# A gated attention and MLP decode step: w2's first half loaded behind wo, and the result summed as two 288-column rows

## The chip, the cores and the metric

The kernel runs on one NeuronCore of a Trainium2 chip. The metric is the device time of one execution in microseconds (us). The kernel before takes 131.41 us, the median of 3 runs (131.40 to 131.53).

## The reference

One token, width 576. Branch A is attention over the last 4096 positions of a cache with 32 query heads, 16 key heads and head width 128. Branch B is an MLP of width 4608 with GELU. A sigmoid gate mixes them.

```python
def _A_ref(x, k_cache, v_cache, wq, wo):          # Hq=32, Hkv=16, Sk=32768, Dh=128
    W = min(4096, max(256, Sk // 4))
    q = (x @ wq).reshape(B, Sq, Hq, Dh).transpose(0, 2, 1, 3)
    k = jnp.repeat(k_cache[:, :, Sk - W:, :], 2, axis=1)
    v = jnp.repeat(v_cache[:, :, Sk - W:, :], 2, axis=1)
    p = softmax(jnp.einsum("bhqd,bhkd->bhqk", q, k) * (Dh ** -0.5))
    o = jnp.einsum("bhqk,bhkd->bhqd", p, v)
    return o.transpose(0, 2, 1, 3).reshape(B, Sq, Hq * Dh) @ wo
def _B_ref(x, w1, b1, w2, b2):
    h = gelu(jnp.einsum("bsd,df->bsf", x, w1) + b1)
    return jnp.einsum("bsf,fd->bsd", h, w2) + b2
g = sigmoid((x * gate_w).sum(-1, keepdims=True))
return g * _A_ref(...) + (1 - g) * _B_ref(...)    # (1, 1, 576), bfloat16
```

## The kernel before

Everything is a product of one row with a large matrix, so the kernel is mostly a stream of loads: w1, wq, four groups of keys (`k_t`), four groups of values (`v_t`), `w2`, `wo`. All of these loads are issued on SP, one after the other. The order of the issues in the program is the order in which the bytes are asked for. A tile that takes over the place (tag) of another one is only loaded when the last reader of the old tile is done.

Each group holds 4 key heads. DVE transposes the keys in two halves (L550), TensorE makes the scores (L572), ACT the exponentials (L609), DVE transposes the probabilities (L621). Then `value_products(g)` (L662) multiplies with group g of the values, `own_sums(g)` (L676, L686, DVE) keeps each head's own part, and `outputs(g)` (L697) collects the heads' columns in `o_ps`. After the last group DVE scales them with the gate into `om` and `om_t` (L769, L778), TensorE turns them into the layout in which wo's rows lie (`ov_ps`, L786 and L793), DVE and ACT copy that to `ov` and `ov_tail` (L802, L804).

The helper `queue("pe", ...)` fixes the order of work on TensorE by hand: each call is issued behind the one before it. The same is done for DVE.

The result is summed in PSUM in the tile `y_ps`. `y_add(vec, row)` multiplies one column of a vector (128 partitions) with one row block of a weight matrix (128 x 576) and adds the 576 products to the sum. It does so as two matmuls in two column groups of the array: columns 0 to 271 on partition 0, columns 272 to 575 on partition 32 in another bank. A "row" in this text is one such call: 36 of them for `w2` (vector `gt`), 31 for `wo` (vector `ov`), 4 for the rest of wo (`wo_tail`, vector `ov_tail`). In the program's order these are: six w2 rows behind the last `value_products`, two behind `outputs(3)`, ten behind the `ov_ps` matmuls, the four tail rows, one dummy matmul (512 columns in fp32 into the unused `spare`, L815), the 31 wo rows, and the second 18 w2 rows.

`w2` is loaded in two halves of 18 rows. The first half is one load (L646, 2592 KB), issued between the second and the third `v_t`; the second half is four loads (L757) of 10, 5, 2 and 1 rows, behind `wo` (L752, 4464 KB). At the end ACT and DVE cast the two parts of the sum into `out_row` on one partition (L828, L829), and SP stores it (L830).

Of the kernel before, what the change touches and what calls it, by code (L numbers as in the profile page):

```python
# [9 lines left out]
FP32 = mybir.dt.float32  # L10
BF16 = mybir.dt.bfloat16
I32 = mybir.dt.int32
ACT = mybir.ActivationFunctionType
ALU = mybir.AluOpType
# [4 lines left out]
def kernel(  # L19
# [15 lines left out]
    nc = tc.nc  # L35

    P = 128
    D = 576
# [9 lines left out]
    NJ = FH // P  # L48
    NF = 2 * NJ
    NI = 2 * D // P  # L50
    QH = Hq * Dh // 2
    DH = 272
    SCALE = 1.0 / (Dh**0.5)

    def first_load_ahead(nc):
# [153 lines left out]
    const = ctx.enter_context(tc.tile_pool(name="const", bufs=1))  # L209
# [3 lines left out]
    ps_y = ctx.enter_context(tc.tile_pool(name="ps_y", bufs=1, space=bass.MemoryType.PSUM))  # L213
# [29 lines left out]
    c0 = 0  # L243
    for base, pattern, keep in (
# [6 lines left out]
        n = 1  # L251
# [8 lines left out]
        out=is0[:], in0=low[:], scalar1=0.0, scalar2=None, op0=ALU.is_equal  # L260
    )
    alt = is0[:, 0 : 2 * NI].rearrange("p (i t) -> p i t", t=2)
    ones = const.tile([P, P], FP32, name="ones")
# [12 lines left out]
        out=at31,  # L276
        in_=at31,
# [8 lines left out]
        out=hi5[:],  # L286
        in_=ones[:, 0:5],
# [7 lines left out]
        out=hi5[:],  # L295
        in_=hi5[:],
# [6 lines left out]
    c0 = 2 * NI  # L303
    hi16 = const.tile([P, 16], FP32, name="hi16")
    nc.gpsimd.tensor_scalar(
        out=hi16[:], in0=is0[:, c0 : c0 + 16], scalar1=-SCALE, scalar2=None, op0=ALU.mult
# [6 lines left out]
        out=row_of,  # L313
        in_=row_of,
# [9 lines left out]
        out=foreign[:],  # L324
        in_=foreign[:],
# [11 lines left out]
        out=xdup.rearrange("p (d t) -> p d t", t=2),  # L337
        in_=x_row.rearrange("p (d o) -> p d o", o=1).to_broadcast([1, D, 2]),
    )
    xs_ps = ps_m.tile([P, NI, 1], FP32, name="xs_ps", tag="m")  # L340
    for i in range(NI):
        nc.tensor.matmul(  # L342
            xs_ps[:, i, :],
            lhsT=xdup[:, i : 2 * D : NI],
            rhs=ident[0:1, 0:1],
            start=(i == 0),
            stop=(i == NI - 1),
            skip_group_check=True,
        )
    nc.vector.tensor_tensor(  # L350
        out=x2[:, :, 0:2], in0=xs_ps[:].to_broadcast([P, NI, 2]), in1=alt, op=ALU.mult
# [5 lines left out]
        out=junk_row,  # L357
        in0=x_row,
        in1=gw_row,
# [15 lines left out]
    b2g = const.tile([1, D], FP32, name="b2g")  # L375
# [2 lines left out]
    nc.scalar.activation(out=gh[:, 0, :], in_=hi5[:], func=ACT.Copy, scale=g_t[:, 0:1])  # L378


    y_ps = ps_y.tile([64, 1024], FP32, name="y_ps")
    y_out = (y_ps[0:1, 0:DH], y_ps[32:33, 512 : 512 + D - DH])

    def y_add(vec, row, start=False, stop=False):
        for s in range(2):
            last = nc.tensor.matmul(  # L386
                y_out[s],
                lhsT=vec,
                rhs=row[:, DH:D] if s else row[:, 0:DH],
                start=start,  # L390
                stop=stop,
                skip_group_check=True,
            )
        return last

    y_add(ones[0:1, 0:1], b2g[0:1, :], start=True)


    QZ = 24
# [30 lines left out]
    for c0, src, q in ((0, h_s[0], 2), (1024, h_s[1], 2), (2048, h_m, 4)):  # L430
        n = 1024 if q == 2 else 256
        nc.vector.transpose(  # L432
            out=turned[:, c0 : c0 + n],
            in_=src[:].rearrange("p (q l j) -> p q j l", q=q, l=32),
# [3 lines left out]
    for j0, j1, b0 in ((0, 16, 0), (16, NJ, 64)):  # L438
        nc.tensor.matmul(
            hp_ps[:, :, :, j0:j1].rearrange("p q t j -> p q j t"),  # L440
            lhsT=same32,
            rhs=turned_t[:, b0 : b0 + 4 * (j1 - j0), :],
            start=(j0 == 0),
            stop=True,
            skip_group_check=True,
        )
    hacc = const.tile([P, NF], FP32, name="hacc")
    for q in range(4):
        quad = slice(32 * q, 32 * q + 32)
        nc.scalar.copy(  # L450
            out=hacc[quad], in_=hp_ps[quad, q, :, :].rearrange("p t j -> p (t j)")
# [6 lines left out]
        out=poly[:],  # L458
        in0=z2[:],
# [12 lines left out]
    gt = const.tile([P, NF], BF16, name="gt")  # L472
    nc.vector.scalar_tensor_tensor(
        out=gt[:], in0=hacc[:], scalar=omg[:, 0:1], in1=r_t[:], op0=ALU.mult, op1=ALU.mult
# [11 lines left out]
    for c in range(2):  # L486
        nc.vector.transpose(  # L487
            out=q_turned[:, 1024 * c : 1024 * c + 1024],
            in_=q_s[c][:].rearrange("p (h l b) -> p h b l", l=32, b=2),
# [4 lines left out]
        lhsT=same32,  # L494
        rhs=q_turned[:].rearrange("p (h j l) -> p h j l", h=16, j=4)[:, :, :, 0:2],
        start=True,
        stop=True,
    )
    for b in range(4):
        quad = slice(32 * b, 32 * b + 32)  # L500
        at = QZ + 32 * b
# [4 lines left out]
            out=diag[:, :, :, 0:8],  # L506
            in_=qj_ps[quad].rearrange("p j g q -> p g j q"),
# [11 lines left out]
    p_t = const.tile([P, 32, 32], BF16, name="p_t")  # L519
# [6 lines left out]
    def queue(engine, emit):  # L526
        if engine in issued:
            with tc.issue_after(issued[engine].ins):
                issued[engine] = emit()
        else:  # L530
            issued[engine] = emit()

    def load(name, tag, cache, g):
        tile_ = big.tile([P, NCK, Dh], BF16, name=name, tag=tag)
        src = cache[0, HB * g : HB * g + HB, Sk - W : Sk, :].rearrange(
            "b (k c) d -> k b (c d)", k=NKP
        )
        nc.sync.dma_start(out=tile_[:].rearrange("p c d -> p (c d)"), in_=src)
        return tile_
# [103 lines left out]
    w2_t = big.tile([P, NF, D], BF16, name="w2_t", tag="B")  # L643
    w2_src = B_w2.rearrange("(b p j) n -> p b j n", b=2, j=NJ)
    v_t = [load("v_t", "CD"[g], A_v_cache, g) for g in range(2)]
    nc.sync.dma_start(out=w2_t[:, 0:NJ, :], in_=w2_src[:, 0])  # L646
    v_t.append(load("v_t", "A", A_v_cache, 2))
    wo_src = A_wo.rearrange("(h d) n -> h d n", d=P)
    tail = wo_src[:, 4 * RW : P, :]
    for h0, h1, at, k in ((0, 16, 0, 4), (16, Hq, 32, 4)):  # L650
        load_tail = nc.sync.dma_start(
            out=wo_tail[at : at + h1 - h0].rearrange("h j n -> h (j n)"),
            in_=tail[h0:h1].rearrange("h j n -> h (j n)"),
# [40 lines left out]
    def outputs(g):  # L694
        queue(
            "pe",
            lambda: nc.tensor.matmul(  # L697
                o_ps[:, 8 * g : 8 * g + 8],
                lhsT=summed[g][:],
                rhs=same8[:, 0:8],  # L700
                start=True,
                stop=True,
            ),
        )
# [9 lines left out]
        out=ls[:],  # L714
        in0=same8[:, 0:8].rearrange("p (o q) -> p o q", o=1).to_broadcast([P, NG, 8]),
        in1=sums[:].to_broadcast([P, NG, 8]),
        op=ALU.mult,
# [5 lines left out]
    spare = acc3[:, 512:1024]  # L723
# [5 lines left out]
            t_ps, lhsT=ones[:], rhs=ls[:].rearrange("p g q -> p (g q)"), start=True, stop=True  # L729
# [7 lines left out]
        out=rgh[:],  # L737
        in0=rg[:].to_broadcast([P, Hq, 5]),
        in1=gh[:].to_broadcast([P, Hq, 5]),
        op=ALU.mult,  # L740
# [12 lines left out]
        out=wo_t[:].rearrange("p r n -> p (r n)"),  # L753
        in_=wo_src[:, 0 : 4 * RW, :].rearrange("h (a r) n -> h a (r n)", a=4),
    )
    for j0, j1 in ((0, 10), (10, 15), (15, 17), (17, 18)):
        nc.sync.dma_start(out=w2_t[:, NJ + j0 : NJ + j1, :], in_=w2_src[:, 1, j0:j1, :])  # L757

    def w2_rows(f0, f1):
        for f in range(f0, f1):  # L760
            queue("pe", lambda: y_add(gt[:, f : f + 1], w2_t[:, f, :]))

    w2_rows(0, 6)
    outputs(3)
    o_all = o_ps.rearrange("p (h o) -> p h o", o=1)
    om = const.tile([P, Hq, 4], BF16, name="om")
# [3 lines left out]
            out=om_t.rearrange("p (u h) -> p u h", u=2)[:, :, 0:16],  # L770
            in0=o_ps.rearrange("p (u h) -> p u h", u=2),
            in1=rgh[:, :, 4].rearrange("p (u h) -> p u h", u=2),
            op=ALU.mult,
# [5 lines left out]
            out=om[:], in0=o_all.to_broadcast([P, Hq, 4]), in1=rgh[:, :, 0:4], op=ALU.mult  # L779
        ),  # L780
    )
    w2_rows(6, 8)
    ov_ps = ps_m.tile([P, RO + 4], FP32, name="ov_ps", tag="m")
    queue(
        "pe",
# [4 lines left out]
    for a in range(4):  # L790
# [4 lines left out]
                lhsT=om[:].rearrange("p h a -> p (h a)"),  # L795
                rhs=at31[:, a, :],
                start=(a == 0),
                stop=(a == 3),
# [4 lines left out]
    ov_tail = const.tile([48, 4], BF16, name="ov_tail")  # L803
    nc.scalar.copy(out=ov_tail[:], in_=ov_ps[0:48, RO : RO + 4])  # L804

    w2_rows(8, NJ)
    late = [(ov_tail, j, wo_tail[:, j, :]) for j in range(4)]
    late.append(None)
    late += [(ov, r, wo_t[:, r, :]) for r in range(RO)]
    late += [(gt, f, w2_t[:, f, :]) for f in range(NJ, NF)]  # L810
    for n, item in enumerate(late):
        if item is None:
            queue(
                "pe",
                lambda: nc.tensor.matmul(  # L815
                    spare,
                    lhsT=ones[:],
                    rhs=p_t[:].rearrange("p c k -> p (c k)").bitcast(FP32),
                    start=True,
                    stop=True,  # L820
                ),
            )
            continue
        vec, at, row = item
        queue("pe", lambda: y_add(vec[:, at : at + 1], row, stop=(n == len(late) - 1)))

    out_row = const.tile([1, D], BF16, name="out_row")
    nc.scalar.copy(out=out_row[:, DH:D], in_=y_out[1])  # L828
    nc.vector.tensor_copy(out=out_row[:, 0:DH], in_=y_out[0])  # L829
    nc.sync.dma_start(out=out.rearrange("a b d -> (a b) d"), in_=out_row[:])  # L830


# [28 lines left out]
```

## Time and profile before

| what | value |
|---|---|
| median of 3 runs | 131.41 us (131.40 to 131.53) |
| the profiled execution | 131.67 us |
| span of its records | 130.3 us |
| mean granted TensorE clock | 0.817 |
| DMA | 53.67 MB, mean 412 GB/s over the span |
| busy TensorE, VectorE, ScalarE, GpSimd | 79.3, 61.0, 11.5, 10.0 us |

The span runs from the first to the last instruction that the profiler recorded; the execution is 1.4 us longer. PE is TensorE, PEld its weight loads, DVE VectorE, ACT ScalarE, POOL GpSimd, SP SyncE, and SPq its DMA issues. A group such as `L386 PE MATMUL ... x72` gives a line of the kernel, an engine, an operation and how many there are. "PEclk" is the clock that TensorE was granted, as a share of the full one. A line in the timeline gives start, duration, engine, line and operation, and in brackets the idle time ahead of it with what ended it.

### The profile page before, as it was taken

The page shows a single profiled execution, that of the slowest core. Times are in us where ns is not written, and L with a number is a line of the kernel's source. Part 1 is how long each engine was busy: PE and PEld are TensorE (multiplying, and loading weights), DVE is VectorE, ACT ScalarE, POOL GpSimd, SP SyncE. Part 2 cuts the span into 40 slices and gives each one's busy share as a digit, 9 for nine tenths or more (in the row PEclk, how much of TensorE's full clock was granted, in tenths as well). Part 3 has the DMA queues.
Part 4 walks back from the last instruction along what each step waited for, and adds up shares of the span by engine and source line. Part 5 has one row for each costly group of instructions (what it writes and reads, how often), then busy time and mean ns, then how long its engine had stood idle before and what let it go on. Part 6 is the DMA issues. An engine that isn't in the chain of part 4 may idle for free.

```text
span 130.3 us, 1142 instructions
## 1 busy us (share of the span) xinstructions
PE 79.3 (61%) x538; PEld 26.2 (20%) x412; DVE 61.0 (47%) x50; ACT 11.5 (9%) x27; POOL 10.0 (8%) x32
## 2 busy tenths in 40 slices
PE   0003899297106996859949946995300840789794
PEld 0003012110100221211211210132200320245572
DVE  0030006215199769999999995145900050051001
ACT  3032100300300000030003003003000000000001
POOL 7009800100000000000000000000010000000000
PEclk9999999658755799985999995599655577579999
DMA  7999999899899999989989989999989999898970
GB/s 249 404 437 432 475 419 475 364 473 473 362 453 473 408 402 473 433 382 473 443 372 473 453 362 473 391 458 443 443 372 477 444 392 475 384 493 356 407 294 15
DMA packets 2503, 53.67 MB, mean 412 GB/s; under 512 B 286, under 2 KB 418, under 8 KB 708
## 3 DMA queue, kind: packets, MB, share of 16 engines
q1 hardware_dynamic: 2490, 53.61, 96.3%
q8 instruction: 3, 0.05, 0.2%
q10 hardware_dynamic: 10, 0.01, 0.0%
HBM read 53.62 MB, written 0.00 MB: 412 GB/s over the span
## 4 chain that ended last, share of the span: by engine, by line
DMA 60%; DVE 21%; PE 13%; issue 5%; ACT 0%; DVEq 0%
DMA k_t<-in_A_k_cache_dram 31%; DMA wo_t<-in_A_wo_dram 25%; DVE kt L550 15%; PE y_ps L386 5%; PE s_ps L572 5%; DMA rows<-in_A_x_dram 5%; DVE m L588 3%; DVE pt L621 2%; PE s_ps L662 1%; PE acc L662 1%; DVE mr L591 1%; ACT out_row L828 0%; PE mt_ps L597 0%; DVE negm L605 0%; DVEq L550 0%
## 5 line engine op out<-in xcount | busy, mean ns | idle before, releaser
L572 PE MATMUL s_ps<-kt,qz_flat 128*128 128x512 bf16 x128 | 35.3, 436 | 15.1 <-DVE kt L550 8.3
L550 DVE STREAM_TRANSPOSE kt<-k_t 128x4096 f32<-128x4096 f32 x8 | 35.3, 4432 | 4.8 <-DMA k_t<-in_A_k_cache_dram 4.8
L662 PE MATMUL s_ps<-v_t,pt 128*32 128x512 bf16 x96 | 9.1, 547 | 12.0 <-DMA v_t<-in_A_v_cache_dram 12.0
L572 PEld LDWEIGHTS <-qz_flat 128*128 128x128 bf16 x64 | 7.2, 112 | 40.6 <-issue 40.4
L676 DVE TENSOR_TENSOR own<-s_ps,is 128x512 f32<-128x512 f32 x3 | 2.1, 688 | 18.9 <-PE s_ps L662 18.9
L609 ACT ACTIVATE p_t<-s_ps,negm 128x1024 bf16<-128x1024 f32 x4 | 4.5, 1114 | 50.0 <-DVE negm L605 50.0
L662 PEld LDWEIGHTS <-pt 128*32 128x32 bf16 x128 | 3.7, 117 | 17.5 <-DMA v_t<-in_A_v_cache_dram 12.2
L342 PE MATMUL xs_ps<-ident,rows 1*128 1x1 bf16 x9 | 0.6, 189 | 10.8 <-POOL ident masks.py:199 10.8
L407 PE MATMUL s_ps<-w_t,x 128*32 128x512 bf16 x36 | 6.0, 611 | 1.6 <-DVE x L350 1.6
L588 DVE TENSOR_REDUCE m<-s_ps 128x1 f32<-128x1024 f32 x4 | 4.8, 1195 | 3.9 <-PE s_ps L572 3.9
L386 PE MATMUL y_ps<-w_t,gt 128*1 128x272 bf16 (+1 forms) x72 | 6.3, 304 | 0.0
L407 PE MATMUL s_ps<-wq_t,x 128*32 128x512 bf16 x36 | 4.9, 619 | 2.2 <-DMA wq_t<-in_A_wq_dram 2.2
L621 DVE STREAM_TRANSPOSE pt<-p_t 128x1024 bf16<-128x1024 bf16 x4 | 4.9, 1224 | 2.7 <-ACT p_t L609 2.7
L432 DVE STREAM_TRANSPOSE turned<-s_ps 128x1024 f32<-128x1024 f32 x2 | 2.5, 1249 | 7.3 <-PE s_ps L407 7.2
L829 DVE CAST out_row<-y_ps 1x272 bf16<-1x272 f32 x1 | 0.4, 429 | 10.2 <-PE y_ps L386 10.2
L713 POOL TENSOR_TENSOR ls<-is,sums 128x32 f32<-128x32 f32 x1 | 0.2, 240 | 63.9 <-ACT p_t L609 63.9
L697 PE MATMUL mt_ps<-is,summed 128*128 128x8 f32 x8 | 2.0, 319 | 4.6 <-DVE summed L686 4.6
L386 PE MATMUL y_ps<-wo_t,ov 128*1 128x272 bf16 (+1 forms) x62 | 4.2, 286 | 0.8 <-DMA wo_t<-in_A_wo_dram 0.8
L356 DVE CUSTOM_DVE_ANT_0 rows<-rows 1x576 bf16<-1x576 bf16 x1 | 0.7, 746 | 8.3 <-DMA rows<-in_gate_w_dram 8.3
L386 PEld LDWEIGHTS <-gt 128*1 128x1 bf16 x72 | 4.0, 89 | 1.9 <-issue 0.7
L686 DVE TENSOR_REDUCE summed<-own 128x128 f32<-128x512 f32 x4 | 4.2, 1044 | 0.1
L487 DVE STREAM_TRANSPOSE q_turned<-s_ps 128x1024 f32<-128x1024 f32 x2 | 2.4, 1228 | 3.8 <-PE s_ps L407 3.8
(83 smaller groups left out, 51.9 us busy)
## 6 DMA issues: line engine op xcount, KB each, us to landing
k_t<-in_A_k_cache_dram SPq DMA_DIRECT2D x4, 4096.0 KB, 33.9
v_t<-in_A_v_cache_dram SPq DMA_DIRECT2D x4, 4096.0 KB, 22.8
wq_t<-in_A_wq_dram SPq DMA_DIRECT2D x1, 4608.0 KB, 25.0
wo_t<-in_A_wo_dram SPq DMA_DIRECT2D x1, 4464.0 KB
w_t<-in_B_w_dram SPq DMA_DIRECT2D x1, 2880.0 KB, 14.4
w_t<-in_B_w_dram SPq DMA_DIRECT2D x1, 2592.0 KB, 23.6
w_t<-in_B_w_dram SPq DMA_DIRECT2D x1, 2304.0 KB, 8.3
w_t<-in_B_w_dram SPq DMA_DIRECT2D x1, 1440.0 KB
```

What stands on the lines that cost most here:

```text
L386: last = nc.tensor.matmul(y_out[s], lhsT=vec, rhs=row[:, DH:D] if s else row[:, 0:DH], start=start, stop=stop, skip_group_check=True,)
L407: nc.tensor.matmul(last[n][32 * g : 32 * g + 32], lhsT=vec, rhs=part(n), start=start and g0 == 0, stop=g0 + 4 + g >= len(pieces), skip_gro ...
L432: nc.vector.transpose(out=turned[:, c0 : c0 + n], in_=src[:].rearrange("p (q l j) -> p q j l", q=q, l=32),)
L487: nc.vector.transpose(out=q_turned[:, 1024 * c : 1024 * c + 1024], in_=q_s[c][:].rearrange("p (h l b) -> p h b l", l=32, b=2),)
L550: lambda: nc.vector.transpose(out=kt[g, f][:].bitcast(FP32), in_=keys.rearrange("p c d -> p (c d)").bitcast(FP32),),
L572: last = nc.tensor.matmul(s_ps[g][:, u * 512 : (u + 1) * 512].rearrange("p (c k) -> p c k", k=32), lhsT=qz(g, j, 2 * f + half), rhs=kv[:, ...
L588: queue("dve", lambda: nc.vector.reduce_max(out=m1[:], in_=s_ps[g][:], axis=AX.X))
L609: nc.scalar.activation(out=p_t[:].rearrange("p c k -> p (c k)"), in_=s_ps[g][:], func=ACT.Exp, bias=negm[:, 0:1], scale=SCALE, accum_out=s ...
L621: lambda: nc.vector.transpose(out=pt[:, g, :, :].rearrange("p c q -> p (c q)"), in_=p_t[:].rearrange("p c k -> p (c k)"),),
L662: last = nc.tensor.matmul(acc[g][32 * (c % 4) : 32 * (c % 4) + 32, :], lhsT=pt[:, g, c, :], rhs=v_t[g][:, c:NCK:32, :], start=(c < 4), sto ...
L676: lambda: nc.vector.tensor_tensor(out=own[:], in0=acc[g].rearrange("p (c d) -> p c d", c=4), in1=same_c.rearrange("p (c o) -> p c o", o=1) ...
L686: lambda: nc.vector.tensor_reduce(out=summed[g][:], in_=own[:].rearrange("p c d -> p d c"), axis=AX.X, op=ALU.add,),
```

## The change

- The first half of `w2` is no longer loaded between the second and the third `v_t`, but behind `wo` and ahead of the four pieces of the second half. Its 18 rows move behind the wo rows on TensorE, so none is left among the last attention steps.
- Of the dummy matmuls there are now four of 512 columns ahead of the wo rows, one of 512 between wo and w2, and one of 256 between the halves of w2.
- The sum lies as two rows of 288 columns on partitions 0 and 32 of one bank (`y_ps`). The last eight w2 rows go through `y_late`: columns 0 to 151 of each row are added to `y_ps`, columns 152 to 287 go into a second bank (`yb_ps`). Ahead of them ACT copies columns 152 to 287 of the sum so far into `y_part`.
- The first of the late rows (and the bias row) use 32 equal weight columns, so that all 32 partitions of a group are written.
- At the end ACT casts 152 columns and DVE adds `y_part` to 136 columns of `yb_ps`, each over 33 partitions; the store takes partitions 0 and 32, 288 elements each.

```diff
-    DH = 272
+    DH = D // 2
+    DA = 152
...
-    y_ps = ps_y.tile([64, 1024], FP32, name="y_ps")
-    y_out = (y_ps[0:1, 0:DH], y_ps[32:33, 512 : 512 + D - DH])
+    y_ps = ps_y.tile([64, DH], FP32, name="y_ps")
+    yb_ps = ps_y.tile([64, DH - DA], FP32, name="yb_ps")
 
     def y_add(vec, row, start=False, stop=False):
+        wide = vec.shape[-1]
         for s in range(2):
             last = nc.tensor.matmul(
-                y_out[s],
+                y_ps[32 * s : 32 * s + wide, :],
                 lhsT=vec,
-                rhs=row[:, DH:D] if s else row[:, 0:DH],
+                rhs=row[:, DH * s : DH * s + DH],
...
-    y_add(ones[0:1, 0:1], b2g[0:1, :], start=True)
+    def y_late(vec, row, start=False, stop=False):
+        wide = vec.shape[-1]
+        for c0, c1, to in ((0, DA, y_ps[:, 0:DA]), (DA, DH, yb_ps[:])):
+            for s in range(2):
+                last = nc.tensor.matmul(
+                    to[32 * s : 32 * s + wide, :],
+                    lhsT=vec,
+                    rhs=row[:, DH * s + c0 : DH * s + c1],
+                    start=start and c0 > 0,
+                    stop=stop,
+                    skip_group_check=True,
+                )
+        return last
+
+    y_add(ones[0:1, 0:32], b2g[0:1, :], start=True)
...
-    nc.sync.dma_start(out=w2_t[:, 0:NJ, :], in_=w2_src[:, 0])
     v_t.append(load("v_t", "A", A_v_cache, 2))
...
+    nc.sync.dma_start(out=w2_t[:, 0:NJ, :], in_=w2_src[:, 0])
     for j0, j1 in ((0, 10), (10, 15), (15, 17), (17, 18)):
         nc.sync.dma_start(out=w2_t[:, NJ + j0 : NJ + j1, :], in_=w2_src[:, 1, j0:j1, :])
...
-    w2_rows(0, 6)
     outputs(3)
...
-    w2_rows(6, 8)
...
-    w2_rows(8, NJ)
     late = [(ov_tail, j, wo_tail[:, j, :]) for j in range(4)]
-    late.append(None)
+    late += [512] * 4
     late += [(ov, r, wo_t[:, r, :]) for r in range(RO)]
+    late += [512]
+    late += [(gt, f, w2_t[:, f, :]) for f in range(NJ)]
+    late += [256]
     late += [(gt, f, w2_t[:, f, :]) for f in range(NJ, NF)]
+    LATE = 8
+    y_part = const.tile([33, DH - DA], FP32, name="y_part")
     for n, item in enumerate(late):
-        if item is None:
+        if isinstance(item, int):
...
-                    spare,
+                    spare[:, 0:item],
...
         vec, at, row = item
-        queue("pe", lambda: y_add(vec[:, at : at + 1], row, stop=(n == len(late) - 1)))
+        column = vec[:, at : at + 1]
+        if n < len(late) - LATE:
+            queue("pe", lambda: y_add(column, row))
+            continue
+        if n == len(late) - LATE:
+            nc.scalar.copy(out=y_part[:], in_=y_ps[0:33, DA:DH])
+            column = column.to_broadcast([P, 32])
+        queue("pe", lambda: y_late(column, row, start=n == len(late) - LATE, stop=n == len(late) - 1))
...
+    out_rows = const.tile([33, DH], BF16, name="out_rows")
+    nc.scalar.copy(out=out_rows[:, 0:DA], in_=y_ps[0:33, 0:DA])
+    nc.vector.tensor_tensor(out=out_rows[:, DA:DH], in0=yb_ps[0:33, :], in1=y_part[:], op=ALU.add)
+    nc.sync.dma_start(out=out.rearrange("a b (s n) -> (a b s) n", s=2), in_=out_rows[0:33:32, :])
```

More of the change, by code (lines that the diff above doesn't have):

```diff
@@ L755 @@
     )
+    nc.sync.dma_start(out=w2_t[:, 0:NJ, :], in_=w2_src[:, 0])
     for j0, j1 in ((0, 10), (10, 15), (15, 17), (17, 18)):
         nc.sync.dma_start(out=w2_t[:, NJ + j0 : NJ + j1, :], in_=w2_src[:, 1, j0:j1, :])
-    def w2_rows(f0, f1):
-        for f in range(f0, f1):
-            queue("pe", lambda: y_add(gt[:, f : f + 1], w2_t[:, f, :]))
-    w2_rows(0, 6)
     outputs(3)
@@ L815 @@
                 lambda: nc.tensor.matmul(
-                    spare,
+                    spare[:, 0:item],
                     lhsT=ones[:],
-                    rhs=p_t[:].rearrange("p c k -> p (c k)").bitcast(FP32),
+                    rhs=p_t[:].rearrange("p c k -> p (c k)").bitcast(FP32)[:, 0:item],
                     start=True,
@@ L824 @@
         vec, at, row = item
-        queue("pe", lambda: y_add(vec[:, at : at + 1], row, stop=(n == len(late) - 1)))
[L827 to L830, printed above, removed]
+        column = vec[:, at : at + 1]
[5 more added lines that the diff above has]
+            column = column.to_broadcast([P, 32])
+        queue(
+            "pe",
+            lambda: y_late(column, row, start=n == len(late) - LATE, stop=n == len(late) - 1),
+        )
+    out_rows = const.tile([33, DH], BF16, name="out_rows")
+    nc.scalar.copy(out=out_rows[:, 0:DA], in_=y_ps[0:33, 0:DA])
+    nc.vector.tensor_tensor(
+        out=out_rows[:, DA:DH], in0=yb_ps[0:33, :], in1=y_part[:], op=ALU.add
+    )
+    nc.sync.dma_start(
+        out=out.rearrange("a b (s n) -> (a b s) n", s=2), in_=out_rows[0:33:32, :]
+    )
 _INS = ['A_x', 'A_k_cache', 'A_v_cache', 'A_wq', 'A_wo', 'B_x', 'B_w1', 'B_b1', 'B_w2', 'B_b2', 'gate_w']
```

## The prediction

> **What bounds the kernel now.** I read the page first: how busy the transfers are.
>
> ```profile
> span 130.3 us, 1142 instructions
> DMA   7999999899899999989989989999989999898970
> q1 hardware_dynamic: 2490, 53.61, 96.3%
> ```
>
> The 16 DMA engines carry 53.61 MB and are busy for 96.3% of the span; only the last two slices drop. The change moves no byte out of that sum, so it can win only where the transfers do not set the end. Next the chain of waits, its end.
>
> ```profile
> 89.91 32.07 DMA wo_t<-in_A_wo_dram
> 121.97 0.04 issue
> 122.01 6.60 PE y_ps L386 x90
> 128.61 0.02 issue
> 128.63 0.40 ACT out_row L828
> ```
>
> By the chain, wo lands at 121.97, TensorE adds rows for 6.60 us, a cast follows. The chain lets TensorE look like the bound of these 6.6 us. The DMA view and the timeline correct that.
>
> ```profile
> w_t<-in_B_w_dram SPq DMA_DIRECT2D x1, 288.0 KB, 36.2
> w_t<-in_B_w_dram SPq DMA_DIRECT2D x1, 144.0 KB, 27.0
> ```
>
> ```profile
> 90.53 11.08 SPq L757 DMA_DIRECT2D w_t<-in_B_w_dram  x4
> 118.10 1.46 PE L386 MATMUL y_ps<-w_t,gt 128*1 128x272 bf16 x20
> 120.09 1.12 PE L815 MATMUL s_ps<-p_t,ones 128*128 128x512 f32 x2
> 121.15 0.08 PEld L386 LDWEIGHTS <-ov 128*1 128x1 bf16 x1 [0.76 <-issue]
> 128.29 0.08 PEld L386 LDWEIGHTS <-gt 128*1 128x1 bf16 x1 [0.16 <-issue]
> 128.60 0.43 DVE L829 CAST out_row<-y_ps 1x272 bf16<-1x272 f32 x1 [10.20 <-PE y_ps L386]
> 129.10 0.28 SPq L830 DMA_DIRECT2D out_dram<-out_row  x1
> ```
>
> The last of the four issues starts at 90.53 + 11.08 - 0.33 = 101.28 (0.33 is the duration of the shortest of the four) and lands 27.0 us later: 128.28. TensorE's last row starts at 128.29. So the last byte sets the end, and TensorE has just caught up (0.16 us idle). Behind the last byte stand 0.3 us of matmul, 0.43 of cast, then 1.16 us from the store's issue to the span's end.
>
> **Part 1, w2's first half goes behind wo.** SP loses one issue between the second and third v_t load and gains it behind wo; the instruction lists show nothing else moved on SP. 4464 KB of wo took 122.01 - 111.46 = 10.55 us from landing to landing, so 2592 KB are 6.1 us. All that was queued behind it comes 6.1 us earlier: the third v_t 101.3 -> 95.2, the fourth 111.46 -> 105.3, wo 122.0 -> 115.9; the first half lands where wo did, at 122.0. The four last pieces keep their bytes ahead of them. Counting back from 128.28 at 0.35 us for 144 KB: 127.9, 127.2, 125.45 for the pieces that end at rows 17, 15, 10. Cover for the moved issue: the third v_t waits for the last key transposes (79.4), while the second v_t keeps the queue filled to about 85 (the old w2 issue of 68.11 landed 23.6 us later, at 91.7, less 6.1). About 5 us are spare, so this costs nothing.
>
> **Part 2, what TensorE loses.** Before, 18 w2 rows ran while TensorE waited for the attention's last sums, and after wo there were 31 + 18 rows. Now all 36 w2 rows and 31 wo rows come behind. A row is two matmuls in two column groups side by side: in the 118.10 line ten rows take 1.46 - 0.29 = 1.17 us for nine steps, 0.130 each for the longer half of 304; a half of 288 gives 0.123.
>
> From the fourth v_t to ov_tail (ACT L804, 118.43 + 0.16) is 118.59 - 111.46 = 7.13 us, so ov_tail is ready at 112.45. Then TensorE has, without a break and at full clock: the four tail rows 0.61 (119.48 to 120.09); **four** dummy matmuls of 512 columns in fp32, where there was one (120.09 to 121.15, 1.06 each): 4.24; 31 wo rows 3.81; a dummy 1.06; 18 w2 rows 2.21; a dummy of 256 columns, 0.64 (its columns halved, its weight loads not); ten w2 rows 1.23. Then the new wait: the ACT copy y_part reads the sum after row 28, and the first late row waits for it, with everything behind it in TensorE's queue. Its price is 0.17 until the row's last column has come out, 0.05 to start, 0.27 for the copy (48x4 took 0.16 and 1x304 0.40, 0.8 ns a column, 136 columns), 0.05 back: 0.54. Then the late rows, four matmuls each (152 and 136 columns): 0.125 a row if columns set it; bounds 0.12 and 0.26 (four steps of 65 ns, the pace of two matmuls in 130). I take 0.125, seven rows to the start of the last: 0.88.
>
> At full clock that ends at 112.45 + 0.61 + 4.24 + 3.81 + 1.06 + 2.21 + 0.64 + 1.23 + 0.54 + 0.88 = 127.67, which is 0.62 us before the last byte. So all is hidden **if the clock is full**. Half of every cold microsecond beyond 1.24 us comes out at the end.
>
> **Part 3, the clock.** The granted clock only changes on a grid of 3.41 us. These are rows on that grid (columns: window, length, busy of PE, PEld, DVE, ACT, POOL, then PEclk).
>
> ```profile
> 78.35:81.77 3.42, 2.38 (x6) 0.43 (x3) 2.09 (x3) 1.21 (x2) 0.00 (x0) 0.50 0.91 393
> 102.25:105.66 3.41, 3.18 (x30) 1.17 (x22) 0.69 (x1) 0.00 (x0) 0.00 (x0) 0.50 1.07 461
> 105.66:109.07 3.41, 0.39 (x2) 0.30 (x2) 1.04 (x1) 0.00 (x0) 0.00 (x0) 1.00 1.00 431
> 109.07:112.49 3.42, 1.03 (x12) 0.45 (x16) 0.00 (x0) 0.00 (x0) 0.00 (x0) 0.50 0.89 383
> 112.49:115.90 3.41, 3.41 (x38) 1.58 (x28) 0.75 (x2) 0.00 (x0) 0.00 (x0) 0.50 1.14 492
> 115.90:119.31 3.41, 2.75 (x37) 1.70 (x29) 1.59 (x4) 0.16 (x1) 0.00 (x0) 1.00 0.82 352
> ```
>
> A window's busy time decides the next one's clock: 3.18 and 3.41 us gave 1.00 next, 0.39 gave 0.50, 2.38 at half clock left 0.50 (81.77 to 85.18 is 0.50 too). Before, the w2 rows filled TensorE from 111.46 to 121.2, and the clock was 1.00 from 115.90 on. After, the fourth v_t's products run 105.3 to 108.9; then until 112.45 only some 0.9 us of small matmuls are left. So at 112.45 the clock is half, and it stays so until a window has been filled.
>
> With the grid as in the profile: half clock from 112.49 to 115.90. Tail rows 1.1, to 113.55; 2.35 us of cold dummies do 1.17 of 4.24; the other 3.07 end at 118.97 (wo has lain there since 115.9). wo rows to 122.78, dummy 123.84, w2 rows 126.05, small dummy 126.69, ten rows 127.92, y_part 128.46, last row starts 129.34 instead of 128.29.
>
> **Part 4, the casts.** Two casts over 33 partitions, 152 columns on ACT and 136 on DVE, beside each other as now. DVE: 0.21 for 32 columns and 0.28 for 128 (L769, L778), so 0.29 instead of 0.43; ACT 0.28, started earlier. The last matmul ends 0.07 + 0.22 after the row's start, as now (0.29). Gain 0.14. The store writes two rows of 576 bytes for one of 1152, bounds -0.1 to +0.15 (the spread of DMA issues in the trace, 0.22 to 0.33 us); I take 0. The first row's 32 wide weights and the two halves of 288 cost nothing I can find (bounds 0 to 0.1).
>
> **Sum.** Late start 1.05, casts -0.14: +0.91. The profiled execution took 131.67 us (span 130.3 and 1.4 around it), 0.26 over the median of 131.41. So 132.58 in a profile, 132.3 as median.
>
> The Trainium skill ("TensorE: Matmul & The Clock Gate", section "Part 1: The HAM clock gate") says that the window is 3413 ns long and free-running, so the kernel's start does not reset it. The trace's grid has that length; one run cannot show whether it moves.
>
> **The rivals.**
> 1. *The grid lies elsewhere* (nothing in the trace ties it to the kernel). A window frees the clock with somewhere between 2.4 and 3.2 busy us. The earliest useful edge is then 1.5 us behind 112.45, cold loss 0.75 - 0.62 = 0.13 late; an edge just too early adds a window, 4.9 to 5.7 cold, up to 2.2 late. With the casts: 131.4 to 133.5, even in between, middle 132.45. For: part 3's rows. Chance 0.40. The page named above would make this the usual case, from one execution to the next.
> 2. *Not slower: TensorE keeps up* (point of decision: under 1.2 us of half clock behind 112.45). Then the last byte still starts the last row, the wait for y_part ends at 127.2 with the piece it waits for anyway, and only the casts count: 131.41 - 0.14 = 131.27, no change that counts. For: at full clock the fillers fit the landings closely (wo rows and dummy end 122.2, w2 lands 122.0). Against: 0.39 busy us in a window gave 0.50 in the next. Chance 0.16.
> 3. *The queue runs dry* between the second and third v_t: each us over the 5 spare costs one. A loss of 1 us (132.3) takes key transposes that end 6 us later; nothing delays them. 0.02.
> 4. *Better than the casts' 0.14*: the store's two rows land on two engines and 0.15 sooner, 131.1. Against: its 1.16 us are far more than 1152 bytes need at 412 GB/s. 0.05.
>
> That the change doesn't do what it says: the instruction lists show SP's new order, six dummies for one, and the wait on ACT ahead of the first late row, so no chance is set aside.
>
> **Numbers.** Forecast with the profile's grid 0.37 (132.0 to 132.6), rivals 0.40, 0.16, 0.02, 0.05. A difference under about 0.2% (0.26 us) cannot be told from none here. Slower: 0.37 + 0.02 + the 0.40 without what falls under +0.26 = 0.78; same 0.14, nearly all rival 2; faster 0.08, rival 4 and the lower edge of 2. The range reaches down to rival 2 (131.2) and up to where the worst grid begins (133.4).
>
> **What would show it.** Right: the third v_t's products near 95.2, the fourth's near 105.3; PEclk 0.50 under the first dummies; no idle before the wo rows, nor before the first late row other than ACT's y_part; the last late row starting well after the last landing near 128.3. Wrong: TensorE idle before the last w2 pieces, dummies at 1.06 us from the first, a gap in the DMA share near 85 us, or late rows at 0.26 us, which alone would add up to 1.

## The result and the profile after

The changed kernel takes 133.41 us as median of six runs (132.20 to 133.95), the kernel before 131.41; the ratio is 1.0138, with a 95% interval of 1.0089 to 1.0188. It is slower, as forecast, but by 2.0 us (1.8 by the ratio) where 0.9 was expected; the median is at the upper edge of the range. Medians are of all runs of a kernel; the ratios here and below leave out runs that took over 1.5% longer than the fastest of the same kernel.

The page first, with the same lines as before.

```profile
span 132.4 us, 1179 instructions
DMA  7999998989998999899899989998998989899910
q1 hardware_dynamic: 2492, 53.61, 94.8%
```

The bytes are the same; the last slices of the DMA line have run down to 1 and 0 (they were 7 and 0): the transfers end and something else goes on. The chain of waits shows what:

```profile
112.09 1.12 PE y_ps L388 x8
113.20 6.34 PE s_ps L829 x8
119.55 3.89 PE y_ps L388 x62
123.44 1.05 PE s_ps L829 x2
124.50 2.30 PE y_ps L388 x36
126.80 0.63 PE s_ps L829 x2
127.42 1.34 PE y_ps L388 x20
128.79 0.27 ACT y_part L844
129.10 0.24 PE y_ps L402 x2
...
130.22 0.07 PE yb_ps L402 x2
130.39 0.29 DVE out_rows L853
```

Before, a transfer (wo, 32.07 us) stood in this place of the chain. Now it is TensorE from the tail rows on, without a gap except the copy y_part. The eight records of L829 are the four fillers: 6.34 us. The timeline gives the ends, to be set beside 128.29 (last row), 128.60 (cast) and 129.10 (store) of before:

```profile
104.90 3.60 PE L677 MATMUL s_ps<-v_t,pt 128*32 128x512 bf16 x32 [4.16 <-DMA v_t<-in_A_v_cache_dram]
113.13 6.42 PE L829 MATMUL s_ps<-p_t,ones 128*128 128x512 f32 x8
119.48 3.96 PE L388 MATMUL y_ps<-wo_t,ov 128*1 128x288 bf16 x62
129.98 0.24 PE L402 MATMUL y_ps<-w_t,gt 128*1 128x152 bf16 x2
130.39 0.29 DVE L853 TENSOR_TENSOR out_rows<-yb_ps,y_part 33x136 bf16<-33x136 f32 x1 [18.54 <-PE yb_ps L402]
130.75 0.59 SPq L856 DMA_DIRECT2D out_dram<-out_rows  x1
```

The wo rows carry no idle bracket: wo had already landed when TensorE came to them. The next lines show the clock's grid (columns as in the prediction: PE's busy time comes after the window's length, the granted clock after POOL's; the line of 94.74 is an earlier window, for comparison further down):

```profile
94.74:98.16 3.42, 3.10 (x32) 1.09 (x32) 0.00 (x0) 0.00 (x0) 0.00 (x0) 0.50 1.00 431
98.16:101.57 3.41, 1.02 (x12) 0.59 (x4) 1.73 (x2) 0.00 (x0) 0.00 (x0) 1.00 0.98 423
108.40:111.81 3.41, 0.95 (x11) 0.50 (x4) 2.30 (x5) 0.00 (x0) 0.00 (x0) 1.00 0.80 346
111.81:115.22 3.41, 3.13 (x11) 1.40 (x12) 0.03 (x1) 0.15 (x1) 0.00 (x0) 0.50 1.02 439
115.22:118.64 3.42, 3.42 (x5) 1.35 (x5) 0.00 (x0) 0.00 (x0) 0.00 (x0) 0.50 1.07 453
118.64:122.05 3.41, 3.41 (x45) 1.91 (x45) 0.00 (x0) 0.00 (x0) 0.00 (x0) 1.00 0.91 386
```

TensorE had little work in the window from 108.40 (0.95 us), and the clock was at half in the next one; it stayed at half for two windows, under nearly all of the four fillers.

The two spans differ by 132.40 - 130.26 = 2.14 us. The last row starts 129.98 - 128.29 = 1.69 later. From that start to the store's issue it is 0.77 us instead of 0.81: -0.04. From the store's issue to the span's end it is 1.65 instead of 1.16: +0.49. The sum is 2.14, so there are two losses: a late TensorE (the wait for y_part is part of that), and a dearer store.

### The profile page after: what moved, and what is told of

It is laid out like the page before. It is cut to its first block, busy times and chain, and to the rows that moved or that the text cites. A ratio compares the mean times of both kernels' runs of the same rounds, so it can differ in the third digit from the quotient of the medians.

```text
span 132.4 us, 1179 instructions
## 1 busy us (share of the span) xinstructions
PE 82.1 (62%) x564; PEld 26.9 (20%) x422; DVE 60.9 (46%) x50; ACT 11.6 (9%) x28; POOL 10.0 (8%) x32
## 4 chain that ended last, share of the span: by engine, by line
DMA 50%; DVE 22%; PE 21%; issue 5%; ACT 0%; DVEq 0%
DMA k_t<-in_A_k_cache_dram 31%; DVE kt L566 15%; DMA v_t<-in_A_v_cache_dram 15%; PE y_ps L388 7%; PE s_ps L829 6%; DMA rows<-in_A_x_dram 4%; PE s_ps L677 3%; PE s_ps L588 3%; DVE m L604 3%; DVE pt L637 2%; PE acc L677 1%; DVE summed L701 1%; PE y_ps L402 1%; DVE mr L607 1%; DVE own L691 1%
## 5 line engine op out<-in xcount | busy, mean ns | idle before, releaser
L588 PE MATMUL s_ps<-kt,qz_flat 128*128 128x512 bf16 x128 | 32.3, 409 | 15.8 <-DVE kt L566 9.0
L829 PE MATMUL s_ps<-p_t,ones 128*128 128x512 f32 (+1 forms) x12 | 8.2, 831 | 0.0
L388 PE MATMUL y_ps<-wo_t,ov 128*1 128x288 bf16 x62 | 4.0, 286 | 0.0
L829 PEld LDWEIGHTS s_ps<-p_t,ones 128*128 128x128 f32 x12 | 3.1, 280 | 4.1 <-issue 4.1
```

The costliest lines, as they stand in the source:

```text
L388: last = nc.tensor.matmul(y_ps[32 * s : 32 * s + wide, :], lhsT=vec, rhs=row[:, DH * s : DH * s + DH], start=start, stop=stop, skip_group_ ...
L588: last = nc.tensor.matmul(s_ps[g][:, u * 512 : (u + 1) * 512].rearrange("p (c k) -> p c k", k=32), lhsT=qz(g, j, 2 * f + half), rhs=kv[:, ...
L829: lambda: nc.tensor.matmul(spare[:, 0:item], lhsT=ones[:], rhs=p_t[:].rearrange("p c k -> p (c k)").bitcast(FP32)[:, 0:item], start=True, ...
```

## The experiments

In all of them the ratio is to the kernel before on the same chip. Two theories stand at the start. One is the prediction's: the fillers run at half clock and make TensorE the bound. The other is that the new sum, its wait and its store are the loss.

**e1, the move alone.** The load and its 18 rows go behind wo; one filler, old sum, old store.

```diff
-    nc.sync.dma_start(out=w2_t[:, 0:NJ, :], in_=w2_src[:, 0])      # behind the second v_t
+    nc.sync.dma_start(out=w2_t[:, 0:NJ, :], in_=w2_src[:, 0])      # behind wo_t
-    w2_rows(0, 6) ... w2_rows(6, 8) ... w2_rows(8, NJ)
-    late += [(gt, f, w2_t[:, f, :]) for f in range(NJ, NF)]
+    late += [(gt, f, w2_t[:, f, :]) for f in range(NF)]
```

> The kernel before with w2's first half loaded behind wo and its 18 rows moved behind the wo rows; one dummy matmul as before, the sum, casts and store as before. Theory (the cold fillers make TensorE late, the move itself is harmless): the transfers still end near 128, the three fillers less give back 3 x 2.1 us at half clock, so TensorE is waiting for the last pieces again: 131.2 to 131.6 us, as before. Rival (rows of one weight column do not raise the clock, so the fillers were needed): wo and w2 rows run at half clock to the end, 0.26 us a row for 67 rows from about 115.5: last row near 132.8 instead of 128.2, some 136 us.

Measured: 131.35 us, ratio 0.9996 (0.9983 to 1.0010). Its timeline:

```profile
113.33 2.07 PE L808 MATMUL s_ps<-p_t,ones 128*128 128x512 f32 x2
115.36 4.97 PE L386 MATMUL y_ps<-wo_t,ov 128*1 128x272 bf16 x62
121.63 2.49 PE L386 MATMUL y_ps<-w_t,gt 128*1 128x272 bf16 x36 [1.30 <-DMA w_t<-in_B_w_dram]
124.99 1.46 PE L386 MATMUL y_ps<-w_t,gt 128*1 128x272 bf16 x20 [0.87 <-DMA w_t<-in_B_w_dram]
126.75 1.38 PE L386 MATMUL y_ps<-w_t,gt 128*1 128x272 bf16 x16 [0.31 <-DMA w_t<-in_B_w_dram]
128.65 0.28 SPq L823 DMA_DIRECT2D out_dram<-out_row  x1
```

The brackets are what to read: TensorE waits 1.30 us for the first half and 0.87 for the next piece. It waits 0.31 more ahead of the last eight rows. TensorE is ahead of the transfers, although it starts at half clock. The wo rows take 4.97 us for 62 matmuls, because they begin cold; the clock rises under them:

```profile
113.62:117.03 3.41, 3.41 (x17) 1.63 (x18) 0.00 (x0) 0.00 (x0) 0.00 (x0) 0.50 0.95 407
117.03:120.44 3.41, 3.30 (x51) 2.52 (x46) 0.00 (x0) 0.00 (x0) 0.00 (x0) 1.00 0.96 406
```

So the move is harmless, and it is also worth nothing that can be measured: the last byte sets the end in either order.

**e2, the move with the changed kernel's fillers**, sum and store of before.

```diff
+    late += [512] * 4          # was one
     late += [(ov, r, wo_t[:, r, :]) for r in range(RO)]
+    late += [512]
+    late += [(gt, f, w2_t[:, f, :]) for f in range(NJ)]
+    late += [256]
```

> The same move with the changed kernel's fillers (four of 512, one of 512, one of 256) and the sum, casts and store of before. Theory (cold fillers): nearly all of the loss is here: 4 x 1.06 us of fillers at half clock, TensorE 0.4 to 2.2 us late; without the wait for y_part (0.5 less) but with rows of 304 instead of 288 (67 x 0.007 = 0.5 more): 132 to 133.6 us by the clock grid's place. Rival (the new sum, its wait and the two-row store are the loss): 131.4 to 131.7 us.

Measured: 132.59 us (131.62 to 133.69), ratio 1.0077 (1.0043 to 1.0112). Fillers alone, against e1, cost 1.2 us by the medians and 1.1 by the ratios. The profile of one of its runs has the four fillers at 113.15 with 6.31 us, as in the changed kernel. Its ten times are spread over 2 us, e1's over 0.6.

**e3, the new sum alone**: y_late, y_part, casts and two-row store of the changed kernel with the order, rows and single filler of before.

```diff
+    nc.sync.dma_start(out=w2_t[:, 0:NJ, :], in_=w2_src[:, 0])   # again ahead of the third v_t
     v_t.append(load("v_t", "A", A_v_cache, 2))
...
+    w2_rows(0, 6) ... w2_rows(6, 8) ... w2_rows(8, NJ)          # again between the attention steps
-    late += [512] * 4
+    late += [512]
```

> The changed kernel's sum, y_part, casts and two-row store with the load order, w2 rows and single dummy of before. In the changed kernel's profile the store's issue took 0.59 us instead of 0.28 and its landing came 1.62 us behind the issue instead of 1.13. Theory that the store's second row costs this 0.5 us always: casts -0.14, late start through y_part up to +0.15, store +0.5: 131.8 to 131.95 us. Rival (0.59 was chance, the store costs nothing): 131.25 to 131.45 us.

Measured: 131.76 us, ratio 1.0018 (0.9999 to 1.0037), that is 0 to 0.5 us slower; by itself this does not decide between the two. The store's issue took 0.59 us again. The copy y_part ran from 127.06 to 127.33; TensorE began the late rows' `yb_ps` halves at 127.03, ahead of it, and their `y_ps` halves at 127.38, behind it. The last row still started at 128.07, right behind the last piece (issued at 101.2, landed 26.8 us later), so here the wait costs nothing.

**e4, one filler in the changed kernel**, all else as it is.

```diff
-    late += [512] * 4
+    late += [512]
     late += [(ov, r, wo_t[:, r, :]) for r in range(RO)]
-    late += [512]
     late += [(gt, f, w2_t[:, f, :]) for f in range(NJ)]
-    late += [256]
```

> The changed kernel with one filler of 512 columns in all (ahead of the wo rows, as before) instead of four, one and a half. Theory (cold fillers are the loss): TensorE waits for the last pieces again; what is left is casts -0.14 and the store's +0.5 if that is real: 131.75 us, or 131.3 if it is not. Rival (the fillers are needed for the clock): later than the changed kernel, 134 us or more. Rival (the wait for y_part and the late rows are the loss): unchanged near 133.4 us.

Measured: 131.83 us, ratio 1.0021 (1.0007 to 1.0036): some 1.5 us of the changed kernel's loss is gone with the fillers. TensorE waits for pieces again (1.61 and 1.09 us in the brackets of its timeline). The remaining 0.1 to 0.5 us fits what the store should cost.

**e5, two fillers instead of four.**

```diff
-    late += [512] * 4
+    late += [512] * 2
```

> The changed kernel with two fillers of 512 columns ahead of the wo rows instead of four; the later fillers of 512 and 256 stay. Theory (cold fillers make TensorE late): two fillers less are 4.3 us at half clock, more than the changed kernel's 1.9 us between the last landing and the last row, but the wo rows may then run at half clock themselves; TensorE is late by 0 to 0.5 us, what is left is the store: 131.8 to 132.2 us. Rival (the fillers between and behind the rows, or the wait for y_part, cost as much as the first four): 132.6 us or more.

Measured: 131.73 us, ratio 1.0026 (1.0017 to 1.0036), just below the range that was expected. So two of the first four fillers make the difference to 133.4; the fillers of 512 and 256 further on, which stay here, cost nothing that shows against e4 (1.0021). In its profile the two fillers are cold throughout and end at 117.06, the wo rows then run at full clock, and the ten rows that y_part waits for start at 125.11, where the changed kernel's start at 127.36. The clock's grid does not lie at the same place in these profiles: the clock came back at 117.0 in e1, e4 and e5, at 118.4 in e2 and at 118.6 in the changed kernel. Part of the 2.25 us is therefore the grid; what the fillers cost rests on the medians, not on one pair of timelines.

**e6, only one row stored.** e4, whose store writes the first 288 columns and leaves the second half of the output out.

```diff
-    nc.sync.dma_start(out=out.rearrange("a b (s n) -> (a b s) n", s=2), in_=out_rows[0:33:32, :])
+    nc.sync.dma_start(out=out.rearrange("a b (s n) -> (a b s) n", s=2)[0:1, :], in_=out_rows[0:1, :])
```

> The one-filler version of the changed kernel (label e4) whose store takes the first row of 288 alone: the second half of the output is not written. Theory (the second row, two partitions 32 apart, costs the store 0.5 us): issue 0.28 instead of 0.59 us and landing 1.1 us behind it, 131.3 us against 131.83. Rival (576 bytes or the source on 33 partitions are the cost): issue near 0.59 and 131.8 us.

Measured: 131.17 us, ratio 0.9981 (0.9972 to 0.9990). Against e4's ratio that is 0.4%, 0.5 us. The end of e4's timeline, then of e6's:

```profile
128.60 0.29 DVE L851 TENSOR_TENSOR out_rows<-yb_ps,y_part 33x136 bf16<-33x136 f32 x1 [16.27 <-PE yb_ps L402]
128.96 0.59 SPq L854 DMA_DIRECT2D out_dram<-out_rows  x1
```

```profile
128.39 0.29 DVE L851 TENSOR_TENSOR out_rows<-yb_ps,y_part 33x136 bf16<-33x136 f32 x1 [16.28 <-PE yb_ps L402]
128.75 0.27 SPq L854 DMA_DIRECT2D out_dram<-out_rows  x1
```

The issue costs 0.59 us with the second row and 0.27 without, and the span ends 1.65 us behind the issue (130.61 - 128.96) against 1.15 (129.9 - 128.75). Size is not the reason: the one row has 576 bytes too, and the kernel before stored all 1152 bytes as one row with an issue of 0.28. Whether it is the second row itself or its place 32 partitions away was not tried, nor were two stores of one row each. e6 is also 0.2 us faster than the kernel before; the casts account for 0.04 of that (below), the rest is not placed.

**e7, more fillers, earlier.** The changed kernel with all its fillers and two more, where TensorE is idle behind the last value products.

```diff
+    filler(512)
     outputs(3)
+    filler(256)
```

> The changed kernel with two fillers MORE: one of 512 columns behind the fourth value products and one of 256 behind outputs(3), where TensorE is idle, so that the clock is granted before the four fillers begin; all else as in the changed kernel. Theory (the clock, not the count of fillers): the four fillers run at 1.06 us each instead of up to 2.13, although the kernel has more work: 131.8 to 132.6 us. Rival (the amount of filler work): 133.4 us or more, by up to 0.3 us for the added delay of outputs(3).

Measured: 131.87 us, ratio 1.0029 (1.0018 to 1.0041). More work, and by the medians 1.5 us faster than the changed kernel. The grid and the four fillers (L843) show why:

```profile
105.61:109.02 3.41, 3.18 (x32) 0.93 (x24) 0.18 (x1) 0.00 (x0) 0.00 (x0) 0.50 0.92 398
109.02:112.43 3.41, 2.37 (x13) 1.06 (x12) 2.17 (x5) 0.15 (x1) 0.00 (x0) 1.00 1.11 482
112.43:115.85 3.42, 3.42 (x15) 1.65 (x16) 0.00 (x0) 0.00 (x0) 0.00 (x0) 1.00 0.89 381
```

```profile
112.97 3.70 PE L843 MATMUL s_ps<-p_t,ones 128*128 128x512 f32 x8
116.60 3.96 PE L388 MATMUL y_ps<-wo_t,ov 128*1 128x288 bf16 x62
121.91 2.37 PE L388 MATMUL y_ps<-w_t,gt 128*1 128x288 bf16 x36 [0.29 <-DMA w_t<-in_B_w_dram]
```

The window after the value products now has 2.37 us of work instead of 0.95, the clock stays at 1.00, and the same four fillers take 3.70 us instead of 6.42. This separates the clock from the amount of work, and the clock it is. That holds for six of the nine runs (131.64 to 131.95 us, mean clock 0.856 to 0.893), and the ratio is theirs. The other three took 133.92 to 135.24 us, at mean clocks of 0.807 to 0.834. Runs in which the clock was not granted early, so that the fillers were cold, would look like that; none of the three was profiled.

**e8, no filler at all.**

```diff
-    late += [512]              # of e4
```

> The changed kernel without any filler. Theory (wo rows of one weight column raise the clock by themselves, as in e1, where the clock rose at 117.0 under cold rows): TensorE idles from about 113.4 to wo's landing at 115.4, runs wo rows at half clock until a grid window is filled (3.4 to 6.8 us, 1.7 to 3.4 us lost, of 3.8 us of slack ahead of w2's first half and 1 us more ahead of the last pieces) and is on time for the last pieces: 131.75 us, as with one filler. Rival (a filler with all 128 weight columns is needed to raise the clock): rows at half clock to the end, the last near 131 instead of 128.2: 134 us or more.

Measured: 131.80 us (131.66 to 132.91), ratio 1.0031 (1.0009 to 1.0053). Rows of one weight column raise the clock by themselves, only later (the two grid lines hold nothing but such rows):

```profile
116.22:119.63 3.41, 3.41 (x32) 1.88 (x30) 0.00 (x0) 0.00 (x0) 0.00 (x0) 0.50 1.02 436
119.63:123.05 3.42, 3.22 (x54) 2.16 (x52) 0.00 (x0) 0.00 (x0) 0.00 (x0) 1.00 0.95 397
```

```profile
112.36 1.12 PE L388 MATMUL y_ps<-zeros,ov_tail 48*1 48x288 bf16 x8 [0.47 <-ACT ov_tail L814]
115.49 5.97 PE L388 MATMUL y_ps<-wo_t,ov 128*1 128x288 bf16 x62 [2.01 <-DMA wo_t<-in_A_wo_dram]
121.66 2.37 PE L388 MATMUL y_ps<-w_t,gt 128*1 128x288 bf16 x36 [0.20 <-DMA w_t<-in_B_w_dram]
125.14 1.39 PE L388 MATMUL y_ps<-w_t,gt 128*1 128x288 bf16 x20 [1.11 <-DMA w_t<-in_B_w_dram]
```

The wo rows take 5.97 us, and TensorE is just in time for w2 (0.20 us of waiting). So the four fillers heated something that needed no heat: the slack ahead of the first half of w2 covers cold rows. It does not always: two of the ten runs took 132.5 and 132.9 us, with the two lowest mean clocks (0.792 and 0.793, the others 0.804 to 0.869).

No version beats the kernel before. e1 is level with it, and e6 writes half of the output. Taken apart, the losses do not quite add up: fillers 0.77% (e2) and the new sum with its store 0.18% (e3) leave 0.4% of the changed kernel's 1.38%. The wait for y_part would be worth that (0.51 us in the changed kernel's profile, nothing in e3, where TensorE was not late), but no run takes that wait out alone, and the interval of the changed kernel is as wide as what is missing.

## Why the prediction was right or wrong

**The bound and the moved load: right.** The value products started at 104.90 (105.3 predicted), the tail rows at 112.09 (112.45), wo had landed before the rows came to it, and no gap opened in the queue (the DMA line shows 9 or 8 in every slice from 80 to 120 us).

**The mechanism: right.** TensorE late behind cold fillers, shown by e1 against e2, by e4 and e5, and from the other side by e7. Rival 2 (TensorE keeps up) is what e4, e5, e7 and e8 are.

**The cold time: too short.** Part 3 put the half clock from 112.49 to 115.90, 3.4 us. It lasted from 111.81 to 118.64; under the work from 112.09 on that is 6.5 us. The grid lay elsewhere (rival 1). On top of that, the window 111.81 to 115.22 had 3.13 us of busy time and did not raise the clock, which the prediction's bound of 2.4 to 3.2 allowed but its 4.9 to 5.7 us for the worst grid did not use: that bound took the edge as missed when it came less than 1.5 to 2.3 us behind 112.45, while here one 3.1 us behind the start was missed. So the term that was mis-sized is part 3's cold time: 3.4 us in the forecast, 5.7 at most in rival 1, 6.5 measured. Its rule that a window's busy time decides is not the whole of it either. In the same profile 3.10 us of value products (94.74 to 98.16) raised the clock, and 3.13 us of tail rows and fillers did not; in e2 it was 2.83 us (94.54 to 97.96) against 2.98 (111.61 to 115.02). The two windows that failed both begin with some 1.0 us of tail rows, which use 48 partitions and one weight column. Whether such rows count for less was not tried.

The rule of the Trainium skill ("TensorE: Matmul & The Clock Gate", section "Part 1: The HAM clock gate") that the window does not reset when the kernel starts agrees with the profiles: the clock came back at 115.90 before, at 118.64 after and at 117.03 in e1, which are not whole windows of 3.41 us apart. The six runs of the changed kernel would fit it: 132.20 us at a mean clock of 0.883, 132.61 at 0.870, 133.67 to 133.95 at 0.845, 133.15 at 0.819. That the grid's place makes this spread is not shown, since only one of the six (133.67) has a profile, and the mean clock alone does not order them.

**The fillers: too dear at full clock.** 1.06 us each was read from a lone one. Back to back they are 3.70 for four in e7, some 0.9 each. That is 0.54 us less than the 4.24 of the sum, and it hid part of the error in the cold time. With the measured start (112.09), 3.70 for the fillers, 6.55 us at half clock and 0.51 for y_part, the prediction's sum gives 130.0 for the last row, and 129.98 was measured: the terms are the right ones, their sizes were off.

**The late rows: right.** y_part cost 0.51 us (from 128.59, ten rows of 0.123 behind their start at 127.36, to 129.10; 0.54 predicted), and seven late rows took 129.98 - 129.10 = 0.88, as predicted.

**The casts: a third of the gain.** 0.14 was predicted; row start to store issue gained 0.04. The DVE operation took 0.29 as predicted, but it started 0.41 us behind the row's start (130.39 - 129.98) instead of 0.31 (128.60 - 128.29): the last matmuls' records end at 130.28, and DVE began 0.11 behind that, where the cast of before began 0.04 behind its matmul. Why was not tried.

**The store: left at nothing.** Part 4 took 0 with bounds of -0.1 to +0.15 from the spread of the DMA issues in the trace; it cost 0.49, outside the bounds. No transfer of two rows 32 partitions apart was in the trace of before, and the bounds should have said so. Rival 4 expected the opposite sign, and falls with the store's 1.65 us against 1.16.

**The sum.** In profiles: predicted +0.91, measured 133.67 - 131.67 = 2.00. The late start was 1.69 instead of 1.05, the casts -0.04 instead of -0.14, the store +0.49 instead of 0; the rest is what lies around the spans. That the median still lies at the edge of the range is partly luck. The fillers' price was 0.54 too high, and the store's missing 0.49 about cancels that; and the edge of 133.4 itself does not follow from the working, by which the worst grid begins at 131.41 + 1.83 - 0.14 = 133.1 and ends at 133.5. Of the chances, "slower" comes to 0.37 + 0.02 + 0.35 = 0.74 by rival 1's even spread, not 0.78.

## What to carry to other kernels

When work is moved out of a stage that a wait has left empty, look at what that stage did for the clock: the rows that used to fill it were the warm-up for what follows, and here a window with 0.95 us of work was followed by 6.8 us at half clock. Fillers do no harm where they run in idle time ahead of the critical work and keep the clock up (six of nine runs of e7); where they stand cold in its queue they cost. And if there is slack, the work itself warms the clock: no filler at all (e8, 131.80 us) did as well as the most fillers (e7, 131.87). The last store of a kernel is paid in full, so cast time won by spreading a result over partitions has to be set against what the store then costs: here 0.04 against 0.49.

## What the runs showed of the hardware

- A store of two rows of 576 bytes from partitions 0 and 32 took 0.59 us to issue, one row 0.27 to 0.28; from issue to the span's end 1.65 us against 1.15 (e4, e6 and the kernel before).
- A window of 3.13 us busy (tail rows of one weight column on 48 partitions, then fillers) left the clock at half, and so did one of 2.98 us in e2; 3.10 us of value products in the same changed kernel, 2.83 us of them in e2 and 3.18 us in e7 raised it. So the busy time that the profile counts does not decide alone; what else decides was not tried.
- Rows that use one of 128 weight columns do raise the clock (e8, where nothing else ran from 116.22 to 119.63): 62 matmuls took 5.97 us there, 3.96 at full clock.
